# Row slots taken in order and transposes moved from TensorE to DMA, in a linear-attention and ELU-MLP kernel

## The chip, the cores and the metric

One Trainium2 (trn2) chip, one of its cores. The metric is the device time of one launch in microseconds (us); each kernel was run several times, and medians are quoted. The profile is one execution, and its span leaves out about 2 us that the device time includes. Engines are named as in the profile: PE is TensorE (PEld its weight loads), DVE is VectorE, ACT is ScalarE, POOL is GpSimd, SP is the sequencer that issues most DMAs here (SPq: the time in which it issues them).

## The reference

```python
# q, k, v: (8 batches, 8 heads, 576 rows, 64), float32
kv  = np.einsum('bhsd,bhse->bhde', k, v)
o   = np.einsum('bhsd,bhde->bhse', q, kv)
rms = np.sqrt(np.mean(o * o, axis=-1, keepdims=True) + 1e-06)
x   = (o / rms * g_norm).transpose(0, 2, 1, 3).reshape(4608, 512)
h   = x @ w_in                                  # 512 -> 2048
g   = np.where(h > 0, h, np.exp(np.minimum(h, 0)) - 1)   # ELU
out = g @ w_out                                 # 2048 -> 512
```

The 4608 rows of x are worked in nine groups of 512. Per group the first product (x by w_in) and the second product (g by w_out) are 64 matmuls each, with 512 columns, in bf16.

## The kernel before

Groups 0 to 7 are the first 512 rows of each batch; group 8 gathers the last 64 rows of all eight. Batch T+1's attention is woven into the loop of group T, while the second product of group T-1 fills TensorE. First, q and the normalised rows must lie with features on partitions, and TensorE does both turns, 16 transposes each per group, through PSUM:

```python
def q_t():                                    # q, rows -> features on partitions
    qt_ps = at_tile(BF16)...
    for p in range(NPAIR):
        q_t_mm(bf["q", T], qt_ps, p)          # 4 transposes on PE each
    ...
    nc.vector.tensor_copy(out=qT[:, 0:2, :], in_=qt_ps[:, 0:2, :])
    nc.scalar.copy(qT[:, 2:4, :], qt_ps[:, 2:4, :])

def x_t():                                    # the normalised rows, the same way
    ...                                       # 16 transposes on PE into xt_ps
    nc.vector.tensor_scalar(
        out=x[:, 0:2, :], in0=xt_ps[:, 0:2, :], scalar1=g_col, scalar2=None, op0=ALU.mult
    )
    nc.scalar.mul(x[:, 2:4, :], xt_ps[:, 2:4, :], g_col)   # the gain rides on the copy
```

Second, the order of the loop. `mm1` starts the first product of one eighth of the features and its Exp on ACT; `rest()` finishes the ELU on DVE:

```python
# start = {"kv": 0, "q": 1, "se0": 2, "se1": 4, "x": 6}: the step after which a piece of attention(T+1) comes
for i in range(8):
    rest = mm1(T, i, ...)          # 8 matmuls, then Exp on ACT
    for name in early.get(i, ()):
        at[name]()                 # sums and inverse roots of attention(T+1)
    second[i]()                    # 8 matmuls of group T-1's second product
    rest()                         # ELU on DVE: min/subtract, then max
    for name in late.get(i, ()):
        at[name]()                 # kv, q, se, mul, x of attention(T+1)
```

So the transposes of x and the copies out of PSUM with the gain are queued one step ahead of the group's last ELU.

## Time and profile before

| | |
|---|---|
| median of three runs | 316.33 us (316.26 to 316.59) |
| profiled span, granted clock | 313.9 us, 0.996 |
| PE busy | 295.2 us, 94% |
| one steady group | 31.53 us, PE busy 31.32 |
| first products of group 1, group 2 begin | 50.17 us (two matmuls at 49.03), 77.64 us |

The page of the profile: busy share of PE and its clock in 40 slices (tenths of full), and the shares of the chain of waits that ended last.

```profile
PE   8677979999999999999999999999999999999992
...
PEclk9999999999999999999999999999999999999998
...
PE 78%; DMA 8%; DVE 5%; ACT 3%; POOL 2%; issue 2%; SPq 1%; DVEq 0%; POOLq 0%
```

TensorE is the limit: from the seventh slice to the last but one it is at 90% or more in each, and 78% of the chain is on it. Windows of the same kernel, in us from the span's start: two steady groups, after the two stages of the start.

```profile
core 0: us, PE busy (x) PEld busy (x) DVE busy (x) ACT busy (x) POOL busy (x), PEclk, DMA share, GB/s
...
21.84:50.17 28.33, 23.89 (x179) 13.12 (x183) 18.54 (x25) 16.94 (x25) 6.47 (x12) 1.00 1.02 217
50.17:77.64 27.47, 26.34 (x184) 13.67 (x186) 18.06 (x22) 17.43 (x24) 16.52 (x28) 1.00 0.61 218
105.39:136.92 31.53, 31.32 (x212) 16.15 (x213) 19.48 (x23) 16.07 (x22) 8.03 (x14) 1.00 0.40 142
```

The steady group leaves TensorE 0.2 us of idle time. The stage between the first products of group 0 and of group 1 has 4.4 us of it, and the next 1.1 us. The timeline at a group boundary (start, duration, engine, line, operation, count; in brackets the idle time of the engine just before, and what ended it):

```profile
135.03 1.89 PE L360 MATMUL o_ps<-w_out_sb,gT 128*128 128x512 bf16 x8
...
136.28 0.43 DVE L336 TENSOR_SCALAR elu_e<-elu_e 128x1024 bf16<-128x1024 bf16 x1 [0.57 <-ACT elu_e L327]
...
136.75 1.06 PE L281 MATMUL at<-ident,xs 128*128 128x128 bf16 x16
...
137.65 1.89 PE L318 MATMUL h_ps<-xT,w_in_sb 128*128 128x512 bf16 x8
```

The 16 transposes cost PE 0.90 us (136.75 to the next matmul at 137.65). The last ELU of the group (DVE, from 136.28) runs beside them; nobody on TensorE waits for it.

### The profile page before, as it was taken

The page shows a single profiled execution, that of the slowest core. Times are in us where ns is not written, and L with a number is a line of the kernel's source. Part 1 is how long each engine was busy: PE and PEld are TensorE (multiplying, and loading weights), DVE is VectorE, ACT ScalarE, POOL GpSimd, SP SyncE. Part 2 cuts the span into 40 slices and gives each one's busy share as a digit, 9 for nine tenths or more (in the row PEclk, how much of TensorE's full clock was granted, in tenths as well). Part 3 has the DMA queues.
Part 4 walks back from the last instruction along what each step waited for, and adds up shares of the span by engine and source line. Part 5 has one row for each costly group of instructions (what it writes and reads, how often), then busy time and mean ns, then how long its engine had stood idle before and what let it go on. Part 6 is the DMA issues. An engine that isn't in the chain of part 4 may idle for free.

```text
span 313.9 us, 4706 instructions
## 1 busy us (share of the span) xinstructions
PE 295.2 (94%) x1905; PEld 149.7 (48%) x1941; DVE 179.5 (57%) x217; ACT 155.4 (50%) x217; POOL 67.1 (21%) x117
## 2 busy tenths in 40 slices
PE   8677979999999999999999999999999999999992
PEld 4444535444554545455545554545455445444440
DVE  4565783487267646764786468646765576544300
ACT  3555954585465445544554455445543554334210
POOL 0465205870082008200720081002000000000000
PEclk9999999999999999999999999999999999999998
DMA  7999959940861076108510861034101010100122
GB/s 254 321 290 256 206 109 388 375 149 2 264 240 67 0 265 238 69 0 278 225 67 2 261 243 67 0 112 92 69 1 67 2 67 2 67 33 34 69 67 67
DMA packets 28597, 42.24 MB, mean 135 GB/s; under 512 B 5536, under 2 KB 17824, under 8 KB 28576
## 3 DMA queue, kind: packets, MB, share of 16 engines
q1 hardware_dynamic: 24352, 37.75, 34.5%
q0 software_dynamic: 4224, 4.19, 8.0%
q8 instruction: 15, 0.25, 0.3%
q14 instruction: 6, 0.05, 0.0%
HBM read 36.70 MB, written 9.44 MB: 147 GB/s over the span
## 4 chain that ended last, share of the span: by engine, by line
PE 78%; DMA 8%; DVE 5%; ACT 3%; POOL 2%; issue 2%; SPq 1%; DVEq 0%; POOLq 0%
PE o_ps L360 36%; PE h_ps L318 34%; DMA w_in_sb<-in_moe_w_in_dram 4%; DVE gT L344 2%; DMA st_k<-in_k_dram 2%; DMA st_v<-in_v_dram 2%; PE at L165 2%; PE at L281 2%; PE at L187 2%; PE at L175 2%; ACT elu_e L327 1%; DVE elu_e L336 1%; POOL v_bf L130 1%; POOL k_bf L130 1%; DVE xs L221 1%
## 5 line engine op out<-in xcount | busy, mean ns | idle before, releaser
L318 PE MATMUL h_ps<-xT,w_in_sb 128*128 128x512 bf16 (+1 forms) x564 | 133.7, 376 | 3.6 <-DMA w_in_sb<-in_moe_w_in_dram 1.7
L360 PE MATMUL o_ps<-w_out_sb,gT 128*128 128x512 bf16 x562 | 134.4, 379 | 0.8
L327 ACT ACTIVATE elu_e<-h_ps 128x1024 bf16<-128x1024 f32 (+1 forms) x74 | 74.0, 1002 | 60.6 <-PE h_ps L318 59.4
L360 PEld LDWEIGHTS <-gT 128*128 128x128 bf16 x576 | 56.3, 98 | 67.2
L336 DVE TENSOR_SCALAR elu_e<-elu_e 128x1024 bf16<-128x1024 bf16 (+1 forms) x73 | 35.3, 484 | 91.1 <-ACT elu_e L327 90.9
L318 PEld LDWEIGHTS <-w_in_sb 128*128 128x128 bf16 x584 | 55.1, 98 | 62.9 <-DMA w_in_sb<-in_moe_w_in_dram 2.4
L344 DVE TENSOR_TENSOR gT<-elu_e,h_ps 128x1024 bf16<-128x1024 bf16 (+1 forms) x66 | 79.5, 1205 | 6.9
L130 POOL CAST q_bf<-st_q 128x512 bf16<-128x512 f32 x32 | 18.9, 628 | 132.9 <-DMA st_q<-in_q_dram 110.6
L370 ACT COPY o_sb<-o_ps 128x512 f32<-128x512 f32 x36 | 21.1, 586 | 25.4 <-PE o_ps L360 25.4
L206 ACT ACTIVATE sq<-at 128x1024 bf16<-128x1024 f32 (+1 forms) x18 | 17.5, 979 | 14.8 <-PE at L187 12.2
L130 POOL CAST v_bf<-st_v 128x512 bf16<-128x512 f32 (+1 forms) x36 | 20.9, 622 | 12.2 <-DMA st_v<-in_v_dram 11.7
L130 POOL CAST k_bf<-st_k 128x512 bf16<-128x512 f32 (+1 forms) x35 | 20.7, 636 | 7.7 <-DMA st_k<-in_k_dram 7.7
L211 DVE TENSOR_REDUCE ss<-sq 128x16 f32<-128x1024 bf16 x16 | 19.5, 1218 | 4.0 <-ACT sq L206 3.8
L221 DVE TENSOR_TENSOR xs<-at,ss 128x1024 bf16<-128x1024 f32 x16 | 19.5, 1218 | 0.6 <-ACT ss L218 0.6
L291 ACT ACTIVATE xT<-at,g_col 128x1024 bf16<-128x1024 bf16 x8 | 8.9, 1114 | 19.4 <-DVE xT L288 19.4
L421 PE MATMUL idle_ps<-zeros,ident 128*128 128x512 bf16 x43 | 12.4, 422 | 1.6 <-POOL ident masks.py:199 1.4
L250 ACT COPY qT<-at 128x1024 bf16<-128x1024 bf16 x8 | 8.1, 1012 | 11.5 <-DVE qT L249 11.5
L165 PE MATMUL at<-v_bf,k_bf 64*128 64x128 bf16 x288 | 10.1, 216 | 2.8 <-DVE v_bf L130 2.0
L165 PEld LDWEIGHTS <-k_bf 64*128 64x128 bf16 x288 | 8.4, 94 | 7.0 <-issue 5.4
L187 PEld LDWEIGHTS <-qT 128*128 128x128 bf16 x128 | 8.4, 98 | 5.9 <-issue 2.5
L187 PE MATMUL at<-bd_kv,qT 128*128 128x128 bf16 x120 | 9.1, 219 | 2.2 <-DVE xs L221 2.2
L241 ACT CAST bd_kv<-at 64x256 bf16<-64x256 f32 x14 | 5.2, 369 | 9.8 <-PE at L165 9.7
(46 smaller groups left out, 107.1 us busy)
## 6 DMA issues: line engine op xcount, KB each, us to landing
st_q<-in_q_dram SPq DMA_DIRECT2D x16, 512.0 KB, 5.5
out_dram<-o_sb SPq DMA_DIRECT2D x16, 512.0 KB, 2.6
st_k<-in_k_dram SPq DMA_DIRECT2D x7, 1152.0 KB, 8.4
st_v<-in_v_dram SPq DMA_DIRECT2D x7, 1152.0 KB, 10.8
w_in_sb<-in_moe_w_in_dram POOLq DMA_DIRECT2D x4, 512.0 KB, 18.4
w_out_sb<-in_moe_w_out_dram POOLq DMA_DIRECT2D x4, 512.0 KB, 20.0
st_k<-in_k_dram SPq DMA_DIRECT2D x2, 576.0 KB, 6.8
st_v<-in_v_dram SPq DMA_DIRECT2D x2, 576.0 KB, 7.8
```

Of the source, the lines that this page charges most:

```text
L130: eng.tensor_copy(out=out_, in_=in_)
L165: nc.tensor.matmul(kv_ps[s][:, u * P : u * P + P], lhsT=bf["k", T][rows, j, 2 * u : 2 * u + 2, :], rhs=bf["v", T][rows, j, 2 * u : 2 * u + ...
L187: nc.tensor.matmul(ov[:, u, :, s, :], lhsT=qT[:, p, j * P : j * P + P], rhs=bd_kv[:, T, p, :], start=True, stop=True,)
L206: nc.scalar.activation(sq, se_ps, AF.Square)
L211: nc.vector.reduce_sum(out=ss, in_=sq.rearrange("p c (h e) -> p (c h) e", h=H), axis=AX.X)
L221: nc.vector.tensor_tensor(out=xs.rearrange("p c (h e) -> p (c h) e", h=H), in0=se_ps.rearrange("p c (h e) -> p (c h) e", h=H), in1=ss.to_b ...
L318: nc.tensor.matmul(h_ps[a][:, cs], lhsT=w_in_sb[:, c, f * P : f * P + P], rhs=x[:, c, cs], start=(c == 0), stop=(c == KC - 1),)
L327: nc.scalar.activation(e[:, lo:hi, :], ps, AF.Exp)
L336: nc.vector.tensor_scalar(out=e[:, lo:hi, :], in0=e[:, lo:hi, :], scalar1=1.0, scalar2=1.0, op0=ALU.min, op1=ALU.subtract,)
L344: nc.vector.tensor_tensor(out=gT[T][:, 2 * i + lo : 2 * i + hi, :], in0=e[:, lo:hi, :], in1=h, op=ALU.add if relu else ALU.max,)
L360: nc.tensor.matmul(o_ps[T, j], lhsT=gT[T][:, f, j * P : j * P + P], rhs=w_out_sb[:, f, :], start=(f == 0), stop=(f == FC - 1),)
L370: nc.scalar.copy(o_sb[T][:, j % 2, :], o_ps.pop((T, j)))
```

## The change

Its intent: take the transposes off TensorE, and shorten the start. Row slots of 64 are taken in order (slot n belongs to batch n // 9), so a group may straddle two batches. Groups 0 and 1 keep features on partitions throughout: the product gives y transposed, a matmul with ones gives the mean of squares, and Ln, Exp and the scaling run over full 1024-column tiles. For groups 2 to 8, q and x are turned by DMA, and the gain becomes two DVE operations of its own. Weights are no longer read beside batch 1; `hold` keeps the fetch of batches 1 and 2 until a piece of w_out has landed. The second product of group 0 runs over all four row tiles (128 rows each) at once. The core of the diff, cut:

```diff
-        def q_t(): ...                # 16 PE transposes, copies on DVE and ACT
-        def x_t(): ...                # 16 PE transposes, gain on DVE and ACT
+    def turn_q(b):
+        qt = qT_tile(b)
+        for s in range(2):
+            nc.sync.dma_start_transpose(
+                out=qt[:, s].rearrange("p u j r -> p (u j) r"),
+                in_=bf["q", b][s * 64 : s * 64 + 64].rearrange("p u j l d -> p (u j l d)"),
+            )
+    ... # in "mul": one dma_start_transpose of x per 128 rows, then
+            def gain():
+                nc.vector.tensor_scalar(          # in place, half of x each
+                    out=xT[T][:, :, cols], in0=xT[T][:, :, cols], scalar1=g_col, ...)
...
+    hold(w_out_sb[0:1, 3, 0:64])      # batch 1 waits for the first slab of w_out
+    for name, src in (("k", k), ("v", v), ("q", q)):
+        fetch(name, src, 1)
...
+    mm2_all(0, 8)                     # group 0's second product, f = 0..7, all 4 row tiles
+    ... # casts of batch 1, its k-v products, q transposes on PE
+    hold(w_out_sb[0:1, 11, 0:64])
+    fetch_all(2)
+    ... # y, square, mean, Ln, Exp, scale: twice, with pieces of mm2(0, ...) between
...
+    fetch_all(3)
+    turn_q(2)
+    ... # group 1's loop
+    early = {3: ("sum0", "inv0"), 5: ("sum1", "inv1")}
+    late = {0: ("kv",), 2: ("se0",), 3: ("mul0",), 4: ("se1",), 5: ("mul1", "gain0"), 7: ("gain1",)}
+    for T in range(2, NT):
+        if T + 2 < B:
+            fetch_all(T + 2)
+        for i in range(8):
+            if i == 0 and T + 1 < B:
+                turn_q(T + 1)
+            rest = mm1(T, i, "BA"[i % 2])
+            ... # early pieces
             mm2_half(T - 1, i)
             rest()
+            ... # late pieces: gain1 comes behind the last ELU
```

## The prediction

> **What bounds the kernel.** The chain of waits that ended last is 78% PE; PE is busy 295.2 of 313.9 us at a granted clock of 0.996. In the steady state (timeline of PE, about 78 to 293 us) PE never waits: a group costs 31.5 us (x transposes at 105.4, next at 136.9). Of that 128 large matmuls at 0.216 us take 27.65; k-v products 1.11, q transposes 0.89, second attention product 0.89, x transposes 0.89. The loop for group 2 starts at 77.6 us; from there PE needs 229 us; the tail after the last product is 5.8 us, and the runs are 2.4 us longer than the profiled span. Before 77.6 PE is held by loads (DMA at 90% or more of its engines until about 42 us) and by the ELU/norm chain on ACT and DVE.
>
> **Removed.** q and x transposes on PE for groups 2 to 8: 7 x 1.78 = 12.5 us of PE, all on the critical path, with their PSUM copies (0.68+0.74 us DVE, 1.01+1.11 us ACT per group). Group 8's 64-row products (1.14 us) become ordinary ones.
>
> **Added.** Per group six DMA transposes (q 590 KB, x 4 x 131 KB), and two gains on DVE (about 0.43 us each, from the bf16 tensor_scalar elu_e). No transpose by DMA is in this trace. The Trainium skill ("DMA: Bandwidth & Descriptors", Latency and other measured facts) gives 261 GB/s; so as an estimate 2.3 us for q, 1 for x, plus about 2 of latency: they should fit, except where they queue behind a 3.5 MB fetch (10.8 us to landing).
>
> **Moved: a new wait.** The second gain comes after the last ELU of a group in DVE's order, and the next group's first matmul needs it. From the start of the last first product: Exp begins at +1.93, DVE at +2.99, ELU ends +4.7, gain +5.1 us. PE arrives at +3.45. I expect a bubble of about 1.7 us at each group boundary. So a steady group takes 27.65+1.11+0.89+0.2 (split slots)+1.7 = 31.5 us, as before: the saving is nearly all given back.
>
> **Start.** First large matmul near 17 us (21.8 before), as weights no longer share DMA with group 1's loads. But those loads now wait for the first slab of w_out (about 26 us), so q of batch 1 lands near 43; the chain y, square, mean, Ln, Exp, scale, twice over 1024 columns, then sets group 1's first product at about 54 us (49 before). The second products fill the gap: 12 us of the first group's 13.8 are done by then. In group 1 little PE filler is left, so ACT and DVE pace it, and at_tile (one buffer) stalls the second se: about 28 us, with perhaps 2 us for a late q transpose. Group 2 would start near 80 to 82 us, not 77.6.
>
> **Sum.** 80 + 229 + 5.8 + 2.4 = 317. I lean a little lower because the bubbles might be shorter: **316 us, range 303 to 325**. Faster by over 2%: 0.35; within 2%: 0.43; slower by over 2%: 0.22.
>
> **What would show it.** Windows: PE no longer above 99% in the steady state but about 94 to 95%. Waits: PE first product <- DVE xT gain, seven times, 1.5 to 2 us. ACT and DVE less busy. Timeline: first product at 17, group 1's at 54, group 2's at 80. Waits of SP: fetches held by v's casts. DMA view: transposes landing in 3 to 5 us.
>
> **What would make it wrong.** The gain landing in time (no bubble): about 305. Group 1 less stalled, group 2 starting at 72 to 75: 5 to 8 us less. Transposes that land in over 6 us, or slow the fetches: bubbles of several us in each group, 325 or more.

## The result, and the profile after

The kernel after took 340.95 us (340.77 to 341.64, four runs), the kernel before in the same rounds 316.46 us (316.26 to 317.41). The ratio is 1.0766, 95% interval 1.0739 to 1.0793: slower by 7.7%. It lies outside the predicted range. (Ratios here are the mean time of one kernel's fast runs over that of the other's fast runs of the same rounds, so not quite the ratio of the quoted medians.)

| | before | after | predicted |
|---|---|---|---|
| span, us | 313.9 | 339.1 | |
| mean granted clock | 0.996 | 0.947 | |
| first large matmul, us | 21.84 | 23.04 | 17 |
| group 1's first product, us | 50.17 | 64.99 | 54 |
| group 2's first product, us | 77.64 | 102.22 | 80 to 82 |
| a steady group, us | 31.53 | 31.49 | 31.5 |

Group 2 begins 24.6 us later, and the span is 25.2 us longer. Everything behind that point therefore takes nearly what it took before. The same views as before; first the page, which shows PE's holes and the lower clock in the first 13 slices (8.5 us each), and DVE and ACT in the last chain.

```profile
PE   6678988781729998999899989998998999899993
...
PEclk9589996995878999999999999999999999999998
...
PE 71%; DVE 7%; ACT 7%; DMA 6%; issue 4%; SPq 2%; POOL 1%; DVEq 0%; ACTq 0%
```

The windows of the two start stages, of group 2 and of a steady group:

```profile
core 0: us, PE busy (x) PEld busy (x) DVE busy (x) ACT busy (x) POOL busy (x), PEclk, DMA share, GB/s
...
23.04:64.99 41.95, 34.31 (x188) 15.89 (x188) 20.97 (x34) 23.82 (x34) 2.78 (x6) 0.92 0.80 215
64.99:102.22 37.23, 20.34 (x122) 9.42 (x124) 17.50 (x22) 15.49 (x21) 14.72 (x30) 0.81 0.65 177
102.22:135.37 33.15, 31.42 (x181) 14.66 (x185) 19.08 (x22) 14.15 (x20) 8.73 (x18) 0.96 0.59 155
135.37:166.86 31.49, 29.76 (x178) 14.28 (x181) 19.14 (x22) 14.14 (x20) 8.51 (x18) 1.00 0.75 182
```

In group 1's stage PE is busy for 6.0 us less than in the same stage of the kernel before (20.34 against 26.34 us), though part of it at half clock, and the stage takes 37.2 us in place of 27.5, at a mean clock of 0.81. In the steady group PE has 1.6 us less to do and needs the same time. The group boundary:

```profile
163.39 1.89 PE L373 MATMUL o_ps<-w_out_sb,gT 128*128 128x512 bf16 x8
...
164.65 0.43 DVE L321 TENSOR_SCALAR elu_e<-elu_e 128x1024 bf16<-128x1024 bf16 x1 [1.70 <-ACT elu_e L312]
165.18 1.22 DVE L329 TENSOR_TENSOR gT<-elu_e,h_ps 128x1024 bf16<-128x1024 bf16 x1
...
166.32 0.48 DVE L282 TENSOR_SCALAR xT<-xT,g_col 128x1024 bf16<-128x1024 bf16 x1
...
166.86 1.90 PE L352 MATMUL h_ps<-xT,w_in_sb 128*128 128x512 bf16 x8 [1.57 <-DVE xT L282]
```

The last ELU (DVE at 164.65 and 165.18) is followed by the gain at 166.32, and only then may the next group's first product start. PE stood idle 1.57 us. The waits of PE that name the two suspects (total, times, longest), and when the transposes land (count, median us from issue to landing):

```profile
PE h_ps L352 <- DVE xT L282: 16.0, 7, 6.6
...
PE at L210 <- DMA qT<-q_bf: 7.6, 2, 7.0
```
```profile
xT<-xs SPq DMA_TRANSPOSE x28, 2.5
qT<-q_bf SPq DMA_TRANSPOSE x16, 5.6
```

Now the part that the prediction missed: group 1's loop on PE, with the issues of SP beside it.

```profile
64.99 1.89 PE L352 MATMUL h_ps<-xT,w_in_sb 128*128 128x512 bf16 x8
...
75.31 0.39 PE L210 MATMUL at<-bd_kv,qT 128*128 128x128 bf16 x4
82.69 0.29 PE L210 MATMUL at<-bd_kv,qT 128*128 128x128 bf16 x1 [7.00 <-DMA qT<-q_bf]
...
83.92 5.63 PE L352 MATMUL h_ps<-xT,w_in_sb 128*128 128x512 bf16 x16
91.57 0.61 PE L210 MATMUL at<-bd_kv,qT 128*128 128x128 bf16 x8 [2.02 <-DVE xs L269]
92.02 3.62 PE L352 MATMUL h_ps<-xT,w_in_sb 128*128 128x512 bf16 x15
102.22 3.28 PE L352 MATMUL h_ps<-xT,w_in_sb 128*128 128x512 bf16 x8 [6.59 <-DVE xT L282]
```
```profile
71.05 0.37 SPq L88 DMA_DIRECT2D st_v<-in_v_dram  x1
71.47 9.55 SPq L301 DMA_TRANSPOSE qT<-q_bf  x2
```

At 75.7 us PE stops in the first attention product of batch 2: q's transposes have not landed. SP had issued them at 71.47, because they stand behind `fetch_all(3)` in its queue, and the v part of that fetch was only issued at 71.05; the two transposes then kept SP for 9.55 us. PE waits 7.00 us, and afterwards 16 matmuls take 5.63 us, where eight take 1.89 us at full clock. Then it waits 2.02 us for a row scaling and 6.59 us for the gain of group 2. These two waits remain when the stall goes (3.30 and 6.66 us in e2), so the stall does not cause them.

The clock itself follows the Trainium skill, "TensorE: Matmul & The Clock Gate", section "Why this matters for your kernels": no idle gaps over about 3 us, or the array falls back to half its clock. This trace agrees for the long gaps: after 7.00 us of idle time the matmuls took 0.35 us each (5.63 over 16) and the eight after the gap of 6.59 us took 3.28 us, while after the 1.57 us gaps of the steady state the clock stayed at 1.00. It is no sharp line, as e3 and e2 show (see the end).

### The profile page after: what moved, and what is told of

The parts are those of the page before. It is cut to its first block, busy times and chain, and to the rows that moved or that the text cites. A ratio compares the mean times of both kernels' runs of the same rounds, so it can differ in the third digit from the quotient of the medians.

```text
span 339.1 us, 4233 instructions
## 1 busy us (share of the span) xinstructions
PE 290.9 (86%) x1617; PEld 136.2 (40%) x1646; DVE 175.1 (52%) x223; ACT 145.7 (43%) x203; POOL 61.0 (18%) x127
## 3 DMA queue, kind: packets, MB, share of 16 engines
HBM read 36.70 MB, written 9.44 MB: 136 GB/s over the span
## 4 chain that ended last, share of the span: by engine, by line
PE 71%; DVE 7%; ACT 7%; DMA 6%; issue 4%; SPq 2%; POOL 1%; DVEq 0%; ACTq 0%
PE o_ps L373 32%; PE h_ps L352 31%; ACT elu_e L312 3%; PE at L157 3%; DMA st_v<-in_v_dram 2%; DVE gT L329 2%; DMA qT<-q_bf 2%; SPq L301 2%; PE at L210 2%; DVE elu_e L321 2%; DVE xT L282 1%; DMA out_dram<-o_sb 1%; ACT rT L197 1%; ACT rT L198 1%; PE qt_ps L431 1%
## 5 line engine op out<-in xcount | busy, mean ns | idle before, releaser
L352 PE MATMUL h_ps<-xT,w_in_sb 128*128 128x512 bf16 (+1 forms) x562 | 137.2, 385 | 19.2 <-DVE xT L282 16.0
L329 DVE TENSOR_TENSOR gT<-elu_e,h_ps 128x1024 bf16<-128x1024 bf16 (+1 forms) x68 | 82.0, 1206 | 7.1
L98 POOL CAST q_bf<-st_q 128x384 bf16<-128x384 f32 (+1 forms) x37 | 18.4, 544 | 150.1 <-DMA st_q<-in_q_dram 150.1
L247 ACT ACTIVATE sq<-at 128x1024 bf16<-128x1024 f32 x14 | 14.3, 1024 | 21.7 <-PE at L210 19.1
L98 POOL CAST v_bf<-st_v 128x384 bf16<-128x384 f32 x36 | 17.0, 519 | 1.2 <-DMA st_v<-in_v_dram 0.9
L98 POOL CAST k_bf<-st_k 128x384 bf16<-128x384 f32 x36 | 16.8, 514 | 1.9 <-DMA st_k<-in_k_dram 1.8
L157 PE MATMUL at<-v_bf,k_bf 64*128 64x128 bf16 x288 | 10.7, 228 | 3.8 <-DVE v_bf L98 3.1
L96 ACT CAST bd_kv<-at 64x256 bf16<-64x256 f32 (+1 forms) x16 | 5.4, 340 | 17.5 <-PE at L157 9.6
L427 PE MATMUL idle_ps<-zeros,ident 128*128 128x512 bf16 x19 | 8.2, 577 | 1.6 <-POOL ident masks.py:199 1.4
L201 DVE SCALAR_TENSOR_TENSOR xT<-y_ps,g_col,rT 128x512 bf16<-128x512 f32 (+1 forms) x5 | 4.3, 855 | 8.0 <-ACT rT L198 8.0
L282 DVE TENSOR_SCALAR xT<-xT,g_col 128x1024 bf16<-128x1024 bf16 x14 | 6.7, 479 | 1.7 <-DMA xT<-xs 1.7
## 6 DMA issues: line engine op xcount, KB each, us to landing
st_k<-in_k_dram SPq DMA_DIRECT2D x7, 1152.0 KB, 10.2
```

Of the source, the lines that this page charges most:

```text
L98: eng.tensor_copy(out=out_, in_=in_)
L157: nc.tensor.matmul(kv_ps[:, s, u * P : u * P + P], lhsT=bf["k", b][rows, j, u], rhs=bf["v", b][rows, j, u], start=(j == 0), stop=(j == RK ...
L247: nc.scalar.activation(sq, se_ps, AF.Square)
L329: nc.vector.tensor_tensor(out=gT[T][:, 2 * i + lo : 2 * i + hi, :], in0=e[:, lo:hi, :], in1=h, op=ALU.add if relu else ALU.max,)
L352: nc.tensor.matmul(h_ps[a][:, cols], lhsT=w_in_sb[:, c, f * P : f * P + P], rhs=xT[T][:, c, cols], start=(c == 0), stop=(c == KC - 1 and l ...
```

## The experiments

Fourteen kernels ran; all gave correct results. The theory had four parts: (A) the gain behind the last ELU costs a boundary wait in each group; (B) q's transposes behind a fetch stall group 1; (C) the serial chain before group 1 starts late; (D) low clock follows from gaps. Rivals were that the holds, the slower loads, or contention from DMA transposes set the time.

### e1_gain: the second gain ahead of the last ELU

```diff
-    early = {3: ("sum0", "inv0"), 5: ("sum1", "inv1")}
-    late = {..., 5: ("mul1", "gain0"), 7: ("gain1",)}
+    early = {3: ("sum0", "inv0"), 5: ("sum1", "inv1"), 7: ("gain1",)}
+    late = {..., 5: ("mul1", "gain0")}
```

> The kernel after, with the second gain of each group from the loop of group 2 on put in front of the last ELU of the group in DVE's order (it was behind it). Theory A, the order makes the bubble: the six boundary waits of PE on the gain of about 1.6 us each vanish, since the transposes land before the last Exp ends; 341 -> 331 (329 to 333). Rival B, the DMA transposes land too late: waits and time unchanged within 2 us. The 6.6 us wait before group 2 is not touched.

Measured: 330.2 us (329.06 to 332.4), ratio 1.0439 (1.037 to 1.0507), 10.7 us less than the kernel after. A boundary in its timeline:

```profile
160.81 1.89 PE L373 MATMUL o_ps<-w_out_sb,gT 128*128 128x512 bf16 x8
...
161.95 0.49 DVE L282 TENSOR_SCALAR xT<-xT,g_col 128x1024 bf16<-128x1024 bf16 x1 [1.58 <-DMA xT<-xs]
162.35 0.42 DVE L321 TENSOR_SCALAR elu_e<-elu_e 128x1024 bf16<-128x1024 bf16 x1
...
162.54 1.89 PE L352 MATMUL h_ps<-xT,w_in_sb 128*128 128x512 bf16 x8
```

The gain runs before the ELU (161.95, then 162.35), and the first product of the next group follows without a gap. Of PE's seven waits for the gain only the one before group 2 is left (6.6 us). The six others were 1.57 us each, 9.4 us together; the rest of the 10.7 us lies within the spread of the runs. Part A holds: only the order cost the time. Group 2 still began at 101.28 us.

### e2_turn_first: q's transposes of batch 2 ahead of the fetch of batch 3

```diff
-    fetch_all(3)
     turn_q(2)
+    fetch_all(3)
```

> The kernel after, with the q transposes of batch 2 issued ahead of the fetch of batch 3 (two lines swapped). Theory: the 7 us stall of PE in group 1 comes from the transposes being held on the SP queue behind that fetch, whose v part waits for its buffer; it goes, with the half clock that follows it: group 2 starts at about 93 us and not 102, 341 -> 332 (330 to 335). Rival: ACT and DVE pace group 1 anyway, the stall only moves, less than 3 us gained.

Measured: 333.45 us, ratio 1.0523 (1.0446 to 1.06), 7.5 us less than after. Group 2 began at 93.60 us instead of 102.22. The wait for q is gone from group 1's stage; those for the row scaling and for the gain stay (SP first, then PE):

```profile
66.44 4.41 SPq L301 DMA_TRANSPOSE qT<-q_bf  x2
```
```profile
82.88 0.61 PE L210 MATMUL at<-bd_kv,qT 128*128 128x128 bf16 x8 [3.30 <-DVE xs L269]
...
93.60 3.59 PE L352 MATMUL h_ps<-xT,w_in_sb 128*128 128x512 bf16 x8 [6.66 <-DVE xT L282]
```

Part B holds for 7.5 us of the loss. Two swapped lines did it.

### e3_idle: 21 more dummy matmuls at the start

```diff
-    idle(4)
+    idle(16)
...
-    idle(1)
+    idle(5)
     q_t_mm(0, 1, range(8), qt_v[:, 1])
+    idle(5)
```

> The kernel after, with 21 more dummy matmuls in PE's gaps of the first 17 us. Theory: the granted clock of 0.5 from 9 to 18 us lies on the start's chain; with it at 1.0 there, the first large product comes 1.5 to 2.5 us earlier, 341 -> 339. Rival: loads and ACT/DVE set the start, under 0.7 us gained.

Measured: 341.32 us, ratio 1.0787, no gain. In its profile the clock was 1.0 from 10 to 20 us and the first large product began at 21.84 us rather than 23.04, but the clock was then 0.66 from 20 to 30 us. That the filler did this is not shown. In the five profiles with unchanged code up to that point (the kernel after, e1, e2, e7, e14) the first large product began anywhere from 21.88 to 23.05 us, at a clock of 0.50 to 0.66 from 10 to 20 us, and e12, with the same PE instructions up to there and no filler, had 0.96 from 10 to 20 us and 0.69 from 20 to 30. The slow stretch of the start thus moves without filler too. What sets the clock between 20 and 30 us was not tested further.

### e4_dma_only: the kernel before, with DMA transposes and gains on DVE for groups 3 to 8 and nothing else

```diff
+    def turn_q(b):                       # q: one DMA transpose per batch
+        qTd[b] = attp.tile([P, J, NPAIR, P], BF16, name="qT", tag="qT")
+        nc.sync.dma_start_transpose(out=..., in_=bf["q", b]...)
...                                       # x: one per 128 rows, after the scaling
+        if T + 1 >= XF and at:           # XF = QF = 3; both gains ahead of the last ELU
+            early.setdefault(7, []).extend(("gain0", "gain1"))
...
             cast_all(T + 1)
+            if T + 1 >= QF:
+                turn_q(T + 1)            # ahead of the fetch of T + 2
         if T + 2 < B:
             fetch(T + 2)
```

> The kernel before, with one part of the change alone: q and x of groups 3 to 8 transposed by DMA, gains on DVE ahead of the group's last ELU, the q transposes issued before the next fetch; groups, start and order of products as before. Theory: the DMA transposes themselves are sound and save 6 x 1.78 = 10.7 us of PE: 316.4 -> 306 (304 to 309), PE still at 99% in the steady state. Rival: they land too late or slow the fetches, 314 or more.

Measured: 305.46 us (304.65 to 306.49), ratio 0.965 (0.9596 to 0.9705): faster than both kernels. TensorE is busy throughout its steady state, with fewer microseconds per group (30 us of it, columns as above):

```profile
136.00:166.00 30.00, 30.00 (x182) 14.41 (x181) 19.84 (x24) 14.13 (x20) 8.12 (x14) 1.00 0.60 185
```

So the transposes by DMA are sound, and in this order they slow nothing that TensorE needs; the rival of contention falls for the steady state. The saving is about 1.8 us for each of six groups, the two sets of transposes that went.

### e10_dma_late_gain: the same with the gain where the change had put it

```diff
-            early.setdefault(7, []).extend(("gain0", "gain1"))
+            late.setdefault(5, []).append("gain0")
+            late.setdefault(7, []).append("gain1")
```

> e4 (before with DMA transposes for groups 3 to 8), with the second gain put behind the last ELU, as the change has it. Theory: this order alone gives the saving back, a wait of PE of some 1.6 us at each of six group boundaries: 305.5 -> 315 (313.5 to 316), about the time of before. Rival: in this kernel the gain is not on the path, 307 or less.

Measured: 316.79 us, ratio 1.0013 (0.9995 to 1.0032): the whole saving is given back by where the gains stand in DVE's order. (The edit moves both; the first one earlier, so it is the second that PE waits for.)

```profile
PE h_ps L346 <- DVE xT L287: 9.8, 6, 1.9
```

Six boundaries, 9.8 us of PE waiting, against 11.3 us between the medians of e10 and e4. The mechanism is shown here in the setting of the kernel before, against e4, from which only this order differs.

### e11_from2: e4, with group 2 by DMA as well

```diff
-    QF, XF = 3, 3
+    QF, XF = 2, 2
...
+    turn_q(2)
     fetch(3)
```

> e4 with group 2 transposed by DMA too (its q transpose issued before the fetch of batch 3). Theory: PE has 1.78 us less to do in group 1's stage, where it is busy 95%: 305.5 -> 304. Rival: ACT and DVE pace that stage or the q transpose lands late, 305 or more.

Measured in five rounds: 309.03 us, ratio 0.9746 (0.9718 to 0.9774), 3.6 us slower than e4; the rival was right. PE pays with a wait for the gain before group 2 and then with half clock (eight matmuls in 3.33 us); that group 1 has too little second-product work left to cover the trip through DMA is likely, not tested:

```profile
80.50 3.33 PE L346 MATMUL h_ps<-xT,w_in_sb 128*128 128x512 bf16 x8 [3.07 <-DVE xT L287]
```

### e6_no_hold: batch 1 is fetched without waiting for w_out

```diff
-    hold(w_out_sb[0:1, 3, 0:64])
```

> The kernel after without the hold that keeps batch 1's fetch back until w_out's first slab has landed (29 us). Rival (my prediction's own reason): the late loads set group 1's start, so it comes several us earlier, 341 -> 336 or less. Theory: PE's order sets it (k and v are cast by 44.3, PE reaches their products at 47.0), so group 1 starts within 1 us of 65 and the time stays within 2 us, unless the weights, now sharing the DMA engines, hold group 0 up.

Measured: 341.87 us, ratio 1.0799. SP had issued the last load of batch 1 by 16.74 us, in place of 30.89. Group 1 began at 63.91 us. That is no gain: unchanged code up to that point put it at 63.35 to 65.76 us in five profiles (the kernel after, e1, e2, e7 and e14), and from the first large product to group 1's it took 41.98 us here, 41.95 in the kernel after. The prediction had blamed this hold for the late start of group 1; the hold is not what sets it. The second hold, ahead of batch 2, was not tested.

### e5_weave: three eighths of the second product between the steps that prepare group 1

```diff
-    mm2_all(0, 8)
+    mm2_all(0, 5)
...
         kv_mm(1, kv_ps, u)
+        mm2_all(5 + u, 6 + u)
...
+    mm2_all(7, 8)                        # after the casts of q
```

> The kernel after, with the last three of the eight slices of the early second product (36 to 47 us) moved in between the k-v products and q transposes of group 1, which so start some 3 us earlier, when their loads are in (44 us). Theory: group 1's preparation is a serial chain that stands behind the second product in PE's order; its first large product comes at about 62 us and not 65, 341 -> 338. Rival, loads or ACT/DVE set the chain's start: under 1 us.

Measured: 338.67 us, ratio 1.0694 (1.0662 to 1.0726). Group 1 began at 62.00 us, 3.0 us earlier than in the kernel after, and 1.4 us ahead of the earliest of the five profiles named under e6; from the first large product it took 39.07 us in place of 41.95. Part C holds to about that size, but PE then waited 7.75 us for q rather than 7.00, so group 2 began only 2.3 us earlier: an earlier arrival waits longer for the same late transposes.

### e7_order1: e2, and group 1's loop in another order

```diff
-    early = {4: ("sum0", "inv0"), 6: ("sum1", "inv1")}
-    late = {2: ("kv",), 3: ("se0",), 4: ("mul0",), 5: ("se1",), 6: ("mul1", "gain0"), 7: ("gain1",)}
+    early = {4: ("mul0",), 5: ("mul1",), 7: ("gain1",)}
+    late = {2: ("kv",), 3: ("se0", "sum0", "inv0"), 4: ("se1", "sum1", "inv1"), 5: ("gain0",)}
```

> e2 (q transposes first) with group 1's loop reordered as well: sums and inverse straight behind each square, scaling ahead of the ELU, the second gain ahead of the last ELU. Theory: the 6.6 us wait of PE for the gain of group 2 is the end of a chain on ACT and DVE of some 26 us; the order takes about 3 us off it, 333.5 -> 330.5. Rival, only the place of the last gain counts: 6 us off, 327.

Measured: 329.44 us, ratio 1.0395 (1.0367 to 1.0423). Group 2 began at 89.67 us, and group 1's stage took 26.3 us instead of 37.2 (28.6 in e2). The wait for the gain fell from 6.66 us (e2) to 2.02 us:

```profile
89.67 3.44 PE L352 MATMUL h_ps<-xT,w_in_sb 128*128 128x512 bf16 x8 [2.02 <-DVE xT L282]
```

The stage is now shorter than the 27.5 us of the kernel before, so all of its excess came of order.

### e14_two_orders: e7 and e1 together

```diff
-    fetch_all(3)
     turn_q(2)
+    fetch_all(3)
...                                    # group 1's order as in e7
-    late = {..., 5: ("mul1", "gain0"), 7: ("gain1",)}
+    early = {..., 7: ("gain1",)}      # as in e1
```

> The kernel after with only orders mended, nothing of the start rewritten: the second gain ahead of the last ELU (e1, which gained 10.7 us), the q transposes of batch 2 ahead of the fetch of batch 3, and group 1's own order (e7, which gained 11.5 us). If the two losses are separate stretches of time they add: 340.9 - 10.7 - 11.5 = 318.7 us, 317 to 320.5, with group 1's first product near 63.4 us, group 2's near 89.7 us, and TensorE without boundary waits after that. Rival: they overlap, and it is 324 us or more.

Measured: 319.18 us (318.33 to 319.85), ratio 1.0081 (1.0059 to 1.0103). The sum of the two gains gives 340.95 - 10.7 - 11.5 = 318.7 us. Group 2 began at 92.26 us, later than expected, as group 1 began at 65.76, at the upper end of the five profiles named under e6. The losses are separate and add: three edits of order, without one instruction added or taken away, give back 21.8 of the 24.5 us.

### e8_chain_first: batch 1's preparation woven into the second product, its casts on POOL

```diff
-    hold(w_out_sb[0:1, 3, 0:64])
...
-    mm2_all(0, 8)
-            cast(name, 1, u, V, low)
-            cast(name, 1, u, A, high)
+    for name in "kvq":
+        for js in (slice(0, 3), slice(3, 6), slice(6, 9)):
+            for u in range(2):
+                cast(name, 1, u, Q, js)      # Q is POOL
+    ... # pairs of mm2_all between the steps of the chain
```

> The kernel after, with no hold, batch 1 cast on POOL, and group 1's preparation started straight after group 0's first products, the early second product woven into its gaps in place of standing before it. Theory: what was lost between group 0 and group 1 (39.4 to 65 us) is this chain laid bare, and with it started at 39.4 and filled, group 1's first large product comes at about 56 us: 341 -> 332 (329 to 334). Rival: the weights, sharing DMA, take it back, 337 or more.

Measured: 341.58 us, ratio 1.0759: a miss. Group 1 began at 65.20 us, as before the edit. One DVE operation, whose median in this run is 0.43 us, took 5.37 us, while POOL cast k and v without a pause (26.14 to 31.8 us), and PE waited 5.25 us behind it:

```profile
26.05 5.37 DVE L321 TENSOR_SCALAR elu_e<-elu_e 128x1024 bf16<-128x1024 bf16 x1 [1.74 <-ACT elu_e L312]
26.14 2.75 POOL L98 CAST k_bf<-st_k 128x384 bf16<-128x384 f32 x6
...
28.84 2.94 POOL L98 CAST v_bf<-st_v 128x384 bf16<-128x384 f32 x6
...
32.80 5.10 PE L352 MATMUL h_ps<-xT,w_in_sb 128*128 128x512 bf16 x16 [5.25 <-DVE gT L329]
```

The Trainium skill, "GPSIMD Engine Reference", section "1. Specifications", says that POOL shares its SBUF interfaces with DVE and contends with some DVE instructions. The 5.37 us fall beside such casts, and in e9, where these casts went to ACT and DVE, the longest of the 73 such operations took 0.79 us. But that POOL's casts alone did it is not shown: e9 also issued them at other times, and later in e8 itself the same operation, inside rows of the same casts for a later batch, took only 0.45 and 0.73 us (at 106.56 and 112.31). The cause of the 5.37 us stays open. Nor was it all that kept group 1 late, since in e9, without it, group 1 began only 2.0 us earlier.

### e9_repaired: e14, with batch 1 fetched and cast early on ACT and DVE, and e8's weaving

```diff
+    for name, src in (("k", k), ("v", v), ("q", q)):
+        fetch(name, src, 1)
     for i, which in zip(range(2, 8), "BABABA"):
         mm1(0, i, which, i in (2, 5))()
+        if i in (4, 6):
+            cast("k", 1, i // 2 - 2, A, all_js)
+            cast("v", 1, i // 2 - 2, V, all_js)
...                                          # otherwise e1 + e7 + the weaving of e8
```

> The kernel after with all repairs: last gain ahead of the ELU (e1), q transposes of batch 2 first and group 1 reordered (e7), and e8's early chain with k, v and q of batch 1 cast on ACT and DVE and not on POOL, as e8's POOL casts held one DVE instruction of group 0 for 5.4 us. Theory: what the change lost is order, not the DMA transposes nor the features on partitions; the parts add up: 341 - 10.5 - 11 - 5 -> 314 (311 to 317), group 1 starting near 60 us. Rival, a loss remains that no order takes off: 320 or more.

Measured: 316.79 us (315.54 to 317.47), ratio 0.9998 (0.9977 to 1.0019): equal to the kernel before. Group 1 began at 63.24 us, not at the expected 60, and group 2 at 90.01.

### e12_quarters: e9, with group 0's second product in row tiles one after another

```diff
-    mm2_all(0..8) over four row tiles at once, six pieces of it before group 1's loop
+    quarters = iter(range(16))               # as the kernel before does it
+    ... # six quarters between the steps of the chain
-    second = {0: (0, 12, 16), 2: (1, 12, 16)}
+    second = (0, 1, 1, 1, 2, 1, 1, 1)        # and ten in and behind group 1's loop
```

> e9 with the last part of the change undone: the second product of group 0 goes row tile by row tile again, six of its sixteen quarters before group 1's first product and ten in and behind its loop, as in the kernel before; in e9 fourteen of sixteen stood before it. Theory: group 1's stage takes some 27 us by its chain on ACT and DVE with or without that work on PE (26.8 us in e9 with little of it, 27.5 in the kernel before with much), so what e9 does ahead of it only delays it: group 1 starts near 58 us and not 63, group 2 near 86 and not 90, 316.8 -> 312.5 (311 to 314). Rival: what comes before group 1 is a chain too, so nothing is gained, 316 or more.

Measured in five rounds: 320.58 us (319.31 to 322.37), ratio 1.0131 (1.0099 to 1.0163). The start came out as expected: 58.25 us for group 1 and 84.72 us for group 2, 5.3 us earlier than e9, of which 1.1 us lie before the first large product (21.08 us, 22.20 in e9). The total did not. The trace shows a new wait in group 2's loop, for q of batch 3, whose transposes stand behind `fetch_all(4)` (PE first, then SP):

```profile
102.56 0.32 PE L219 MATMUL at<-bd_kv,qT 128*64 128x128 bf16 x2 [5.70 <-DMA qT<-q_bf]
...
103.95 3.59 PE L352 MATMUL h_ps<-xT,w_in_sb 128*128 128x512 bf16 x8
```
```profile
88.80 0.46 SPq L88 DMA_DIRECT2D st_v<-in_v_dram  x1
89.36 12.09 SPq L301 DMA_TRANSPOSE qT<-q_bf  x2
```

Two transposes kept SP for 12.09 us, PE waited 5.70 us, and the next eight matmuls ran at half clock (3.59 us). It is part B again, one group later: with group 2 starting earlier, its margin was gone.

### e13_turn_all: e12, with q's transposes ahead of the fetch in the loop too

```diff
+        if T + 1 < B:
+            turn_q(T + 1)
         if T + 2 < B:
             fetch_all(T + 2)
         for i in range(8):
-            if i == 0 and T + 1 < B:
-                turn_q(T + 1)
```

> e12_quarters with one change: in the loop over the later groups the q transposes of the next batch are issued ahead of the fetch of the batch after it, not behind it. Theory: e12 missed its expected time (320.6 us, not 312.5) because the q transposes of group 3, issued at 89.4 us behind the fetch of batch 4 and issued for 12.1 us, stopped TensorE for 5.7 us at 102.6 us and left the clock at half for about 2 us more. Without it: group 2 still starts at about 84.7 us, no wait of TensorE for q^T above 1 us in group 2's loop, and 312 to 313.5 us. Rival: the time went elsewhere (the transposes are slow whatever stands before them, or the delayed fetches stall a later group): 317 us or more.

Measured: 312.15 us (311.21 to 312.32), ratio 0.9861 (0.9841 to 0.9881). The same place in its trace, PE first and then SP:

```profile
96.80 0.39 PE L210 MATMUL at<-bd_kv,qT 128*128 128x128 bf16 x4
...
97.46 1.68 PE L352 MATMUL h_ps<-xT,w_in_sb 128*128 128x512 bf16 x7
```
```profile
87.41 4.25 SPq L301 DMA_TRANSPOSE qT<-q_bf  x2
```

No wait, full clock, and the same two transposes kept SP for 4.25 us instead of 12.09. The theory's 312 to 313.5 us holds and its rival falls. So the change, with its orders mended, batch 1 prepared as in e9 and its second product in row tiles again, is 1.4% faster than the kernel before; the smaller change e4 is 3.5% faster.

| kernel | group 1 begins, us | group 2 begins, us | median, us |
|---|---|---|---|
| before | 50.17 | 77.64 | 316.46 |
| after | 64.99 | 102.22 | 340.95 |
| e2 (q's transposes first) | 65.00 | 93.60 | 333.45 |
| e7 (and group 1's order) | 63.35 | 89.67 | 329.44 |
| e14 (and the gain) | 65.76 | 92.26 | 319.18 |
| e9 (and early casts, woven chain) | 63.24 | 90.01 | 316.79 |
| e13 (and row tiles, and q first everywhere) | 59.18 | 85.22 | 312.15 |
| e4 (only DMA transposes, from group 3) | 50.55 | 78.32 | 305.46 |

"Begins" is the first run of more than two first-product matmuls for group 1; in e13 two came at 56.27 us, in e4 two at 49.41. For group 2 it is the first matmul.

## Why the prediction was wrong

**The steady state was right.** It predicted a bubble of about 1.7 us at each of seven boundaries, behind a gain queued after the last ELU, and a steady group of 31.5 us. Measured: 1.57 us at six of them (6.59 at the first) and 31.49 us, with PE busy for 29.76 us of it, 94.5% (it said 94 to 95). Moving the gain gave 10.7 us (e1), and putting it in the wrong place in e4 took all 11 us back (e10). The medians of the transposes' landing lie just outside "3 to 5": 2.5 us for x, 5.6 for q; the longest, 14.0 us for a piece of q, were not foreseen.

**The step that failed is "Start".** The prediction put group 2's first product at 80 to 82 us; it came at 102.22. It then added 229 us of PE and a 5.8 us tail, 234.8 us; measured from there were 339.1 - 102.2 = 236.9, so 2.1 us of the miss lie behind that point, most of them in group 2 (33.15 us instead of 31.5, with its first matmuls at half clock). Set against the steps that it forecast (17 us, 54 us, and 28 us more to 82), the 20.2 us lost up to that point fall into 6.0, 5.0 and 9.2 us:

1. *First large matmul at 17 us.* It came at 23.04. No wait for w_in is shown there any more, as predicted. But in PE's queue the second half of batch 0's chain stands ahead of it: the k-v product at 18.55 us, y at 20.37, and the two mean matmuls at 21.67 and 22.82, the last of them waiting for the Ln of the first (ACT, 22.08 to 22.77). With the clock at 0.96 to 1.0 from 10 to 20 us, the product still began only at 21.08 (e12) and 21.84 (e3). The prediction took the loads for the only limit.
2. *Group 1's first product at 54 us.* It came at 64.99: 6 us of that came from the start before it, and 5 us more were lost on the way. The reason given, loads held by w_out, is refuted (e6). What stands before group 1 is a serial chain, from y at 52.1 us to the scaling that ends at about 64, and more of the second product: 56 of its 64 matmuls stand ahead of group 1's first product, and only 24 in the kernel before. Both parts were tested: weaving 12 of these matmuls into the steps of the chain gave 1.4 to 3.0 us (e5), and moving 32 of them behind group 1's start, with row tiles, 3.9 us (from the first large product to group 1's: 41.04 us in e9, 37.17 in e12). The last 9 us against the kernel before were not recovered; which part of the chain they belong to is open.
3. *Group 1's stage of 28 us, "with perhaps 2 us for a late q transpose".* It took 37.2. This is the mis-sized term: the late transposes cost a stop of 7.00 us, and slow matmuls behind it, which the sum did not have; taking them away moved group 2 by 8.6 us (e2). Group 1's own order cost another 2.3 us of this stage (28.6 us in e2, 26.3 in e7) and 4.0 us of the time (333.45 and 329.44; 1.65 us of it lie before this stage, within the spread of the start). With both mended the stage takes 26.3 us, below the prediction.

The prediction named the mechanism of point 3 itself ("except where they queue behind a 3.5 MB fetch"), with the fetch's 10.8 us beside it, and then charged 2 us. It also treated the clock as 1.0 throughout, while the mean of group 1's stage was 0.81. And its list of what could go wrong has the start only as better than forecast (group 2 at 72 to 75 us), never as worse.

## What to carry to other kernels

When a transpose or a copy moves from a busy engine to DMA, look where every step behind it stands in its engine's queue, and whether its DMA is issued ahead of the next bulk fetch: here the gain's place was worth 10.7 us (e1) and the q transposes' place 7.5 us (e2), together more than the 11.0 us that the transposes by DMA saved (e4). When a change rewrites both the steady state and the start, run the smallest part alone first (e4 did better than the whole). And cost a stall of TensorE above about 3 us as the stall plus the slow matmuls that mostly followed it here.

## What the Trainium skill lacked or had wrong

- "DMA: Bandwidth & Descriptors", section "Issuing engines are not separate DMA queues", says that the sequencer's time to initiate a DMA is "usually small relative to the DMA itself". For DMA transposes it is not: a pair of q transposes kept SP for 4.25 us when issued ahead of a fetch (e13) and for 12.09 us behind it (e12), and in the kernel after a single one kept it for 2.05 to 9.44 us, 3.6 in the median, against a median landing of 5.6 us. The page has sequencer times for transposes only where it compares trn3 with earlier generations, in cycles.
- The same page has a bandwidth for DMA transposes but no time to landing within a running kernel. Measured here: 2.5 us median for 128 rows of 512 (x), 5.6 us for the pieces of q, mostly half a batch each (from 2.3 to 14.0 us).
- "GPSIMD Engine Reference", section "1. Specifications", names the contention with DVE; that section gives no size, and what other pages say of it is not gone into here. In e8 one 128x1024 bf16 operation of DVE, 0.43 us as a rule, took 0.45 and 0.73 us inside rows of casts on POOL, and once 5.37 us, the cause of which is open.
- "TensorE: Matmul & The Clock Gate", section "Why this matters for your kernels", held, though not as a sharp line: full clock after gaps of 1.57 us; half after 3.07 us in e11 (eight matmuls in 3.33 us) and after 7.00 us; but 16 matmuls in 3.62 us, full clock, close behind a gap of 3.30 us in e2. Part 1 of the same page, which calls the activity window free-running, allows for the gap in e2. And in e3 the clock fell to 0.50 from 20 to 26 us with no gap of PE above 1.88 us since 10.2 us; PE was busy for 2.17 of the 5 us from 17 to 22.
